# Attention feeding a mixture of experts: v loaded by head pairs, weights and the token plan spread over more steps

## The chip, the core and the metric

The kernel runs on one core of one Trainium2 chip. Five engines work beside each other, each through its own instructions in order: TensorE (PE: matmuls, with its weight loads shown as PEld), VectorE (DVE), ScalarE (ACT), GpSimd (POOL) and SyncE (SP). SP computes nothing here; it issues DMAs. POOL and ACT issue some too. The metric is the device time of one execution in microseconds (us), as the median of several runs.

## The reference

Two layers follow each other. The first is attention with rotary positions, for 8 batches of 8 heads, 576 tokens and 64 columns a head:

```python
q_rot, k_rot = (rotate(q), rotate(k))
scores = scale * np.matmul(q_rot, k_rot.transpose(0, 1, 3, 2))
attn = np.exp(scores - np.max(scores, axis=-1, keepdims=True))
attn = attn / (np.sum(attn, axis=-1, keepdims=True) + 1e-09)
return np.matmul(attn, v)
```

Its output, rearranged to 4608 rows of 512 columns, is the x of the second layer. A dense network of two matrices is applied to every row, and beside it one of 8 experts, picked per row by the largest logit and weighted by its probability:

```python
y_dense = np.maximum(x @ w1_dense, 0.0) @ w2_dense
expert_idx = np.argmax(x @ w_gate, axis=1)
for e in range(E):
    mask = expert_idx == e
    h = np.maximum(x[mask] @ w1[e], 0.0)
    y_moe[mask] = gate_w[mask, None] * (h @ w2[e])
return y_dense + y_moe
```

All expert matrices are 512 x 512. All inputs are float32 in the chip's memory.

## The kernel before

**Pairs and steps.** Attention treats two heads at a time: 8 batches times 4 pairs are 32 pairs. `attention()` runs steps i = 0 to 32 of 9 blocks t = 0 to 8. A step is a software pipeline: it makes the first scores of pair i+2 (`s1_block`, PE, whose row maxima DVE reduces to `negm`, L336), the second scores and exponentials of pair i (`s2_strip`, PE L357, ACT L367), and the product with v of pair i-1 (`av_part`, PE L389). DVE then divides by the sums (`av_scale`: the reciprocal at L400 ends a step, L401 writes x for the batch, and L406 adds up the gate's logits after the last pair of a batch). So L400 runs 32 times, and from one to the next is one step. `s1_block` ends with pair 31 in step 29, so that steps 30 to 32 are lighter.

**What a pair needs.** q and k are loaded by SP for two pairs at a time (`stage_load`, L244 and L247: one large DMA and two small ones), q in even and k in odd steps. `stage_rope` rotates them on POOL (L306 to L309) for pair i+5. `stage_transpose` has SP issue a DMA transpose of the result into `qkT` (L318) for pair i+4. `shift_rows` turns the row maxima of pair i+1 into two rows `mT`, which SP writes into `qkT` (L347, two small DMAs): without these rows `s2_strip` of the next step cannot start. All this stands in one queue on SP, in the order in which the program issues it. In a step that is: the two `mT` rows at t = 1, the transpose at t = 2, then at t = 5 the loads of q or k, of v where there are any, and the store of x.

**v.** `vf` holds v of one batch, eight heads in float32. `stage_v(b)` fills it with one 1 MB DMA (L258) and two small ones for the 64 tail rows (L261). It runs once in the head and then in steps 0, 4, 8 up to 24. ACT casts it pair by pair (`cast_v`, L265).

**x and the weights.** `x_store(b)` writes x of a batch to the chip's memory (`xd`, L415 and L416), on SP in steps 5, 9 and so on; that of the last batch is issued by ACT after the last step. `load_w` has POOL issue a DMA that casts a 512 x 512 matrix to bfloat16 (L222): the dense ones in steps 4 and 6, the eight first expert matrices in steps 8, 10 up to 22, the eight second ones in steps 27 to 29.

**The plan.** The rows of the first 6 batches are sorted into 20 tiles of 128 rows by expert while attention still runs. `gate_steps`, `rank_steps` and `plan_steps` give short pieces of work for DVE, POOL and PE; a dictionary `steps[i, t]` says in which block each piece is issued. `rk[3]` to `rk[5]` are three one-hot products on DVE (`oh`, L510), `pl[4]` and `pl[5]` two further ones with a product on POOL (L578), `mm + [fin]` the matmuls and index arithmetic that end the plan. `fetch(g, ...)` then has POOL gather the tiles of a group by indirect DMA (L756), and SP transpose each (L759). Groups 0, 1 and 2 have 1, 3 and 4 tiles; groups 0 to 2 are fetched in steps 31 and 32, and later ones in the second layer, each two groups ahead.

**The second layer.** `run_groups` goes through the tiles: `dense_in` (PE L789, ACT L791) for a group, `expert_in` (PE L798, ACT L801), a transpose on PE (L807), and `out_tile` (PE L816 and L818, DVE L820), from which POOL scatters the rows to the output (L821). The plan for the last two batches is made on the way, from their logits.

Of the kernel before, what the change touches and what calls it, by code (L numbers as in the profile page):

```python
# [21 lines left out]
P = 128  # L22
# [3 lines left out]
def kernel(  # L26
# [12 lines left out]
    nc = tc.nc  # L39
    B, H, S, D = q.shape  # L40
    N, DG = out.shape
    E = moe_w_gate.shape[1]
# [4 lines left out]
    HP = H // 2  # L47
    NP = B * HP
    MAIN = 512
    TAIL = S - MAIN  # L50
# [170 lines left out]
    def load_w(dst, src):  # L221
        nc.gpsimd.dma_start(dst, src.rearrange("(t p) f -> p t f", p=P))  # L222
# [31 lines left out]
            state["qk", g] = early.tile([P, 2, 2, 10, D], f32, tag="qk", bufs=3, name="qk")  # L254
        load(state["qk", g][:, part], (q, k)[part], b, hh)

    def stage_v(b):
        nc.sync.dma_start(vf.rearrange("p u (a j) d -> p (u a) (j d)", a=2)[:, :, 0:4 * D],  # L258
                          v[b, :, 0:MAIN, :].rearrange("h (p j) d -> p h (j d)", j=4))
        for a in range(2):  # L260
            nc.sync.dma_start(vf[64 * a:64 * a + 64, :, 5 * a + 4, :],  # L261
                              v[b, a::2, MAIN:S, :].rearrange("h p d -> p h d"))

    def cast_v(b, u):
        nc.scalar.copy(v16s[b % VB][:, u, :, VA:VA + 2 * D].rearrange("p n (h d) -> p n h d", d=D),  # L265
# [145 lines left out]
    def x_store(b):  # L411
        r0 = b * S
        xn = state["xn", b]
        eng = nc.scalar if b == B - 1 else nc.sync
        eng.dma_start(xd[r0:r0 + MAIN, :].rearrange("(p j) c -> p j c", j=4), xn[:, 0:4, :])  # L415
        eng.dma_start(xd[r0 + MAIN:r0 + S, :], xn[P - TAIL:P, 4, :])  # L416

    def over_experts(k, wp, dst, src, op):

# [196 lines left out]
    def attention():  # L616
        for i in range(2):
            for t in range(9):
                s1_block(i, t)
                if i == 1 and t == 1:  # L620
                    shift_rows(0)
                    for u in range(HP):
                        cast_v(0, u)
        stage_load(3, 0)
        stage_load(3, 1)
        for i in range(3, RA):
            stage_rope(i)
        stage_transpose(3)
        gt = gate_steps(0, wg)
        rk, got0 = rank_steps(0, wg, attn_sums)  # L630
        steps = {(27, 0): gt[0:1], (27, 2): gt[1:2], (27, 4): gt[2:3]}
        AV = (0, 0), (0, 1), (1, 3), (3, 4), (4, 6), (6, 7), (7, 8), (8, 9), (9, 10)
        state["av"] = av_tile(0)
        for i in range(NP + 1):
            for t in range(9):
                if i + 2 < NP:
                    s1_block(i + 2, t)
                if i < NP:
                    s2_strip(i, t)
                if 1 <= i <= NP and t >= 1:  # L640
                    for k in range(*AV[t]):
                        av_part(i - 1, k)
                    if t == 8:
                        av_scale(i - 1)
                if t == (7 if i == 0 else 5) and i + 1 < NP:
                    v_turn(i + 1)
                if i == 0 and t == 2:
                    v_turn(0)
                if i < NP:
                    t0 = 4 if i == 0 else 1  # L650
                    if t == t0:
                        v_gate(i)
                    if t == t0 + 1:
                        v_split(i)
                if t == 1 and i + 1 < NP:
                    shift_rows(i + 1)
                if t == 2 and i + RA < NP:
                    stage_rope(i + RA)
                if t == 2 and i + LA < NP:
                    stage_transpose(i + LA)  # L660
                if i % HP != 1 and (t in (1, 4) if i % HP == 0 else t == 3):
                    u = 2 + t // 4 if i % HP == 0 else i % HP - 2
                    if 1 <= (i + 2) // HP < B and i < NP - 6:
                        cast_v((i + 2) // HP, u)
                if i in (NP - 6, NP - 5) and t in (1, 4):
                    cast_v(B - 1, 2 * (i - NP + 6) + t // 4)
                if t == 5:

                    g, part = divmod(i + 8, 2)
                    if g < NP // 2:  # L670
                        stage_load(g, part)
                    if i % HP == 0 and i // HP + 1 < B:
                        stage_v(i // HP + 1)
                    if i % HP == 1 and i > HP:
                        x_store(i // HP - 1)
                    if i == 4:
                        load_w(w1d, moe_w1_dense)
                    if i == 6:
                        load_w(w2d, moe_w2_dense)
                    if i % 2 == 0 and 8 <= i < 8 + 2 * E:  # L680
                        load_w(w1e[:, (i - 8) // 2], moe_w1[(i - 8) // 2])
                    if i == 25:
                        route_first()
                    if i == 26:
                        route_ranks()
                        route_tokens()
                    if i == NP - RA:
                        early_cm.__exit__(None, None, None)
                        open_late()
                        wa = late["wa"]  # L690
                        pl, mm, fin = plan_steps(0, wa, attn_sums, got0)
                        w2 = [lambda e=e: load_w(late["w2e"][:, e], moe_w2[e]) for e in range(E)]
                        steps[27, 6] = rk[0:1]
                        steps[27, 7] = w2[0:2]
                        steps[28, 0] = rk[1:2] + pl[0:1]
                        steps[28, 2] = gt[3:4] + w2[2:4]
                        steps[28, 4] = pl[1:2]
                        steps[28, 6] = rk[2:3] + w2[4:6]
                        steps[29, 0] = pl[2:4] + w2[6:8]
                        steps[29, 8] = rk[3:4]  # L700
                        steps[30, 1] = rk[4:5]
                        steps[30, 3] = pl[4:5]
                        steps[30, 5] = rk[5:6]
                        steps[30, 6] = pl[5:6]
                        steps[31, 4] = mm + [fin]
                        steps[31, 6] = [lambda: fetch(0, late["first"], 0, 1), lambda: fetch(1, late["first"], 1, 1)]
                        steps[32, 2] = [lambda: fetch(2, late["first"], 2, 1)]
                for st in steps.pop((i, t), ()):
                    st()
            if i < NP:  # L710
                s2_tails(i, 0)
            if i < NP:
                s2_tails(i, 1)
        assert not steps
        x_store(B - 1)

    def attn_sums(shape):
        t = pp.tile([P, 2, 512], f32, tag="av" if len(shape) == 3 else "s1", bufs=1 if len(shape) == 3 else 2, name="sums")
# [6 lines left out]
    late = {}  # L725
# [37 lines left out]
    with tc.tile_pool(name="attn_sb", bufs=2) as ap, \  # L763
# [3 lines left out]
        with tc.manual_schedule():  # L767
# [6 lines left out]
            nc.gpsimd.tensor_copy(ident_b, ident_f)  # L774
            nc.scalar.copy(ident_h, ident_f)
            for i in range(3):
                stage_rope(i)
                stage_transpose(i)
                if i < 2:
                    stage_load(2, i)  # L780
            pad_tails()
            split_gate()
            stage_v(0)
            attention()

    def dense_in(hd, xs, n, ft):
# [139 lines left out]
```

## Time and profile before

| what | value |
|---|---|
| median of 3 runs | 529.09 us (527.86 to 533.12) |
| the profiled execution | 525.88 us, of which its span, first to last instruction, is 524.1 us |
| PE busy in the span | 417.8 us, 80% |
| DVE busy | 357.9 us, 68% |
| POOL busy | 345.2 us, 66% |
| ACT busy | 283.7 us, 54% |
| mean granted clock of PE | 0.947 |

The steps of attention fill the span from about 41 us to 366 us, the second layer the rest. Busy shares are averages over stages with different limits, so the stages are read apart. In a row of the timeline stand the start, the duration, the engine (with a q where it is only the issue of a DMA), the line, the operation, what it writes and reads, and in brackets how long the engine had been idle and who released it. A row of the table by stretches holds the stretch, its length, for PE, PEld, DVE, ACT and POOL the busy time with the number of instructions, then the granted clock, the share of the 16 DMA engines and the GB/s.

### The profile page before, as it was taken

What the parts mean: (1) busy time and instruction counts of PE and PEld (TensorE: products, weight loads), DVE (VectorE), ACT (ScalarE), POOL (GpSimd) and SP (SyncE); (2) the same over time, 40 slices, a digit from 0 to 9 for tenths busy, and PEclk for the clock granted to TensorE, in tenths of its full rate; (3) what the DMA queues carried; (4) which work ended last, traced back from release to release, by engine and by line L of the source; (5) the groups of instructions that cost most, each with busy time, mean ns of one, the idle gap of its engine ahead of it and who ended that gap; (6) DMA issues with size and microseconds to landing.
All of it is one profiled execution on the core that took longest, in us unless ns stands there. A gap on an engine that the chain in (4) does not pass through costs nothing.

```text
span 524.1 us, 11280 instructions
## 1 busy us (share of the span) xinstructions
PE 417.8 (80%) x4220; PEld 258.0 (49%) x4236; DVE 357.9 (68%) x654; ACT 283.7 (54%) x576; POOL 345.2 (66%) x278
## 2 busy tenths in 40 slices
PE   0177998988798888678988978871789899999993
PEld 0023665655565566455655655550344444444551
DVE  7994999989878989859989998820258523332331
ACT  4007887877677777657887865750333223233320
POOL 4999999889499499875988536155024555555232
PEclk9996999999989999979999987995699999999998
DMA  6498879989979979989997479819215544465222
GB/s 181 90 228 186 222 161 191 236 178 227 184 169 169 246 167 228 180 145 219 194 197 174 102 127 131 158 41 182 66 41 141 141 118 128 139 141 148 76 81 82
DMA packets 151431, 81.41 MB, mean 155 GB/s; under 512 B 112560, under 2 KB 146864, under 8 KB 151376
## 3 DMA queue, kind: packets, MB, share of 16 engines
q1 hardware_dynamic: 136384, 56.33, 49.2%
q0 software_dynamic: 14240, 23.73, 21.6%
q8 instruction: 36, 0.59, 0.5%
q10 hardware_dynamic: 752, 0.61, 0.4%
q14 instruction: 19, 0.16, 0.1%
HBM read 52.05 MB, written 14.42 MB: 127 GB/s over the span
## 4 chain that ended last, share of the span: by engine, by line
PE 44%; DVE 15%; DMA 13%; POOL 9%; ACT 6%; issue 5%; SPq 4%; another core or an unknown queue 3%; POOLq 0%; ACTq 0%; DVEq 0%
DVE negm L336 8%; DMA qkT<-mT 7%; PE pe L798 6%; PE pd L789 6%; PE py L816 6%; PE py L818 6%; PE s L357 4%; PE av L389 4%; PE s L334 4%; ACT pm L367 4%; DMA qk<-in_k_dram 4%; POOL ra L306 3%; POOL nat L309 2%; POOL rb L307 2%
## 5 line engine op out<-in xcount | busy, mean ns | idle before, releaser
L336 DVE TENSOR_REDUCE negm<-s 128x1 f32<-128x576 f32 x288 | 211.0, 751 | 32.8 <-PE s L334 27.2
L367 ACT ACTIVATE pm<-s 128x512 f16<-128x512 f32 x288 | 168.7, 598 | 75.9 <-PE s L357 58.9
L334 PE MATMUL s<-qkT 128*128 128x288 bf16 x512 | 111.1, 301 | 38.5 <-DMA qkT<-nat 23.1
L357 PE MATMUL s<-qkT 128*128 128x64 bf16 (+1 forms) x512 | 113.0, 293 | 19.4 <-DMA qkT<-mT 16.4
L389 PEld LDWEIGHTS <-pm 128*128 128x128 f16 x1600 | 88.8, 99 | 68.3 <-issue 40.5
L389 PE MATMUL av<-v,pm 128*128 128x82 f16 x1600 | 102.7, 202 | 11.5 <-DVE v L292 8.8
L306 POOL TENSOR_TENSOR ra<-qk,cosx 128x1152 bf16<-128x1152 f32 x30 | 79.2, 2640 | 33.3 <-DMA qk<-in_k_dram 20.8
L821 POOL DMA_INDIRECT out_dram<-y,put_i x37 | 36.9, 997 | 84.3 <-DVE y L820 49.4
L309 POOL TENSOR_TENSOR nat<-ra,rb 128x1152 bf16<-128x1152 bf16 x30 | 71.9, 2396 | 2.4
L334 PEld LDWEIGHTS <-qkT 128*128 128x128 bf16 x512 | 40.8, 100 | 55.3 <-DMA qkT<-nat 23.1
L791 ACT ACTIVATE hd<-pd 128x512 bf16<-128x512 f32 (+2 forms) x44 | 23.2, 529 | 69.6 <-PE py L816 32.6
L820 DVE COPY y<-py 128x512 f32<-128x512 f32 x37 | 25.5, 690 | 45.3 <-PE py L818 21.7
L789 PE MATMUL pd<-xs,w1d 128*128 128x512 bf16 (+2 forms) x176 | 41.8, 366 | 14.1 <-ACT hd L791 7.3
L357 PEld LDWEIGHTS <-qkT 128*128 128x128 bf16 x512 | 36.0, 98 | 27.3 <-DMA qkT<-mT 11.5
L801 ACT ACTIVATE hn<-pe,gp 128x512 bf16<-128x512 f32 x37 | 25.4, 687 | 43.9 <-PE pe L798 34.9
L756 POOL DMA_INDIRECT xg<-xd,take_i x37 | 36.6, 988 | 15.1 <-issue 11.0
L809 DVE COPY he<-tr 128x512 bf16<-128x512 bf16 x37 | 15.6, 422 | 43.0 <-PE tr L807 33.7
L307 POOL TENSOR_TENSOR rb<-qk,sinx 128x576 bf16<-128x576 f32 x30 | 42.5, 1416 | 0.0
L308 POOL TENSOR_TENSOR rb<-qk,sinx 128x576 bf16<-128x576 f32 x30 | 42.4, 1414 | 0.0
L798 PE MATMUL pe<-w1e,xs 128*128 x139 | 37.8, 384 | 2.3 <-DVE top L454 1.0
L818 PE MATMUL py<-w2e,he 128*128 x147 | 37.8, 379 | 0.0
L816 PE MATMUL py<-w2d,hd 128*128 128x512 bf16 x142 | 36.7, 379 | 0.3
(170 smaller groups left out, 482.2 us busy)
## 6 DMA issues: line engine op xcount, KB each, us to landing
qk<-in_q_dram SPq DMA_DIRECT2D x16, 512.0 KB
qk<-in_k_dram SPq DMA_DIRECT2D x16, 512.0 KB
vf<-in_v_dram SPq DMA_DIRECT2D x8, 1024.0 KB
w1e<-in_moe_w_dram POOLq DMA_DIRECT2D x8, 512.0 KB
w2e<-in_moe_w_dram POOLq DMA_DIRECT2D x8, 512.0 KB
xd<-xn SPq DMA_DIRECT2D x7, 512.0 KB
qk<-in_q_dram SPq DMA_DIRECT2D x32, 32.0 KB
qk<-in_k_dram SPq DMA_DIRECT2D x32, 32.0 KB
```

The costliest lines, as they stand in the source:

```text
L306: eng.tensor_tensor(a, x, cx, AL.mult)
L307: eng.tensor_tensor(s[:, :, :, 0:half], x[:, :, :, half:D], sx[:, :, :, 0:half], AL.mult)
L309: eng.tensor_tensor(nat[:, :, :, 0:D], a, s, AL.add)
L334: nc.tensor.matmul(ps[:, c, 0:CH], lhsT=qT[:, t * P:(t + 1) * P], rhs=kT[:, k0 + c * CH:k0 + (c + 1) * CH], start=True, stop=True)
L336: nc.vector.tensor_reduce(state["negm", i][:, t:t + 1], ps[:, :, 0:CH], axis=AX.XY, op=AL.max, negate=True)
L357: nc.tensor.matmul(out_ap, lhsT=kT[:, s * P:(s + 1) * P], rhs=qT[:, qa if s < 4 else qb], start=True, stop=True)
L367: nc.scalar.activation(state["pm", i][:, ORDER.index(s), 0:MAIN], ps, AF.Exp, scale=float(scale))
L389: nc.tensor.matmul(state["av"][:, h, x * VC:(x + 1) * VC], lhsT=state["pm", i][:, 4 * h + n if n < 4 else 8, q0:q0 + P], rhs=v16s[b % VB][ ...
L789: nc.tensor.matmul(ps[:, 0:n], lhsT=w1d[:, dt, ft * P:(ft + 1) * P], rhs=xs[:, 0:n, dt, :], start=(dt == 0), stop=(dt == DT - 1))
L798: nc.tensor.matmul(ps, lhsT=xs[:, u, dt, :], rhs=w[:, 0, dt, :], start=(dt == 0), stop=(dt == DT - 1))
L816: nc.tensor.matmul(py, lhsT=hd[:, ft, u], rhs=w2d[:, ft, :], start=(ft == 0), stop=False)
L818: nc.tensor.matmul(py, lhsT=he[:, ft], rhs=w[:, 0, ft, :], start=False, stop=(ft == FT - 1))
```

## The change

- `stage_v` takes a pair: one DMA of two heads and two small ones for their tails. In the head it is called four times; in step 0 twice and in steps 1 to 26 once, always for the next pair in line, so that batch b+1 is loaded over the steps in which batch b is worked on.
- The weights: the first dense matrix is loaded in the head, on POOL ahead of the third rotation; the second in step 1; the first expert matrices in steps 3, 6, 10, 14, 18, 22, 26 and 27; the second ones one or two at a time from step 27, block 6, to step 29, block 5.
- The plan begins in step 25 and not 27. Its pieces stand one to two blocks, or one to two steps, earlier; the first one-hot product moves from step 29, block 8, to step 29, block 2, and the closing matmuls from step 31, block 4, to block 3. Constants are prepared in step 24 and not 25.
- The last `x_store` is issued by SP, in block 8 of step 32, ahead of the fetch of group 2, which moves there from block 2. So four tiles (groups 0 and 1) are fetched in step 31 and four in step 32.

```diff
-    def stage_v(b):
-        nc.sync.dma_start(vf.rearrange("p u (a j) d -> p (u a) (j d)", a=2)[:, :, 0:4 * D],
-                          v[b, :, 0:MAIN, :].rearrange("h (p j) d -> p h (j d)", j=4))
+    def stage_v(b, u):
+        nc.sync.dma_start(vf[:, u].rearrange("p (a j) d -> p a (j d)", a=2)[:, :, 0:4 * D],
+                          v[b, 2 * u:2 * u + 2, 0:MAIN, :].rearrange("h (p j) d -> p h (j d)", j=4))
         for a in range(2):
-            nc.sync.dma_start(vf[64 * a:64 * a + 64, :, 5 * a + 4, :],
-                              v[b, a::2, MAIN:S, :].rearrange("h p d -> p h d"))
+            nc.sync.dma_start(vf[64 * a:64 * a + 64, u, 5 * a + 4, :], v[b, 2 * u + a, MAIN:S, :])
...
-        eng = nc.scalar if b == B - 1 else nc.sync
-        eng.dma_start(xd[r0:r0 + MAIN, :].rearrange("(p j) c -> p j c", j=4), xn[:, 0:4, :])
-        eng.dma_start(xd[r0 + MAIN:r0 + S, :], xn[P - TAIL:P, 4, :])
+        nc.sync.dma_start(xd[r0:r0 + MAIN, :].rearrange("(p j) c -> p j c", j=4), xn[:, 0:4, :])
+        nc.sync.dma_start(xd[r0 + MAIN:r0 + S, :], xn[P - TAIL:P, 4, :])
...
-        steps = {(27, 0): gt[0:1], (27, 2): gt[1:2], (27, 4): gt[2:3]}
+        W1 = (3, 6, 10, 14, 18, 22, 26, 27)
+        steps = {(25, 0): gt[0:1], (26, 0): gt[1:2], (26, 4): gt[2:3], (26, 7): rk[0:1]}
...
-                    if i % HP == 0 and i // HP + 1 < B:
-                        stage_v(i // HP + 1)
+                    for n in range(i, i + 2) if i == 0 else (i + 1,):
+                        if HP <= n + HP < NP:
+                            stage_v(n // HP + 1, n % HP)
...
-                    if i == 4:
-                        load_w(w1d, moe_w1_dense)
-                    if i == 6:
+                    if i == 1:
                         load_w(w2d, moe_w2_dense)
-                    if i % 2 == 0 and 8 <= i < 8 + 2 * E:
-                        load_w(w1e[:, (i - 8) // 2], moe_w1[(i - 8) // 2])
-                    if i == 25:
+                    if i in W1:
+                        load_w(w1e[:, W1.index(i)], moe_w1[W1.index(i)])
+                    if i == 24:
                         route_first()
...
-                        steps[27, 6] = rk[0:1]
-                        steps[27, 7] = w2[0:2]
-                        steps[28, 0] = rk[1:2] + pl[0:1]
-                        steps[28, 2] = gt[3:4] + w2[2:4]
-                        steps[28, 4] = pl[1:2]
-                        steps[28, 6] = rk[2:3] + w2[4:6]
-                        steps[29, 0] = pl[2:4] + w2[6:8]
-                        steps[29, 8] = rk[3:4]
-                        steps[30, 1] = rk[4:5]
-                        steps[30, 3] = pl[4:5]
-                        steps[30, 5] = rk[5:6]
-                        steps[30, 6] = pl[5:6]
-                        steps[31, 4] = mm + [fin]
+                        steps[27, 6] = w2[0:1]
+                        steps[27, 7] = rk[1:2] + pl[0:1]
+                        steps[28, 0] = gt[3:4] + w2[1:2]
+                        steps[28, 3] = pl[1:2] + w2[2:4]
+                        steps[28, 4] = rk[2:3]
+                        steps[29, 0] = pl[2:4] + w2[4:6]
+                        steps[29, 2] = rk[3:4]
+                        steps[29, 5] = w2[6:8]
+                        steps[29, 8] = rk[4:5]
+                        steps[30, 2] = pl[4:5]
+                        steps[30, 4] = rk[5:6]
+                        steps[30, 5] = pl[5:6]
+                        steps[31, 3] = mm + [fin]
                         steps[31, 6] = [lambda: fetch(0, late["first"], 0, 1), lambda: fetch(1, late["first"], 1, 1)]
-                        steps[32, 2] = [lambda: fetch(2, late["first"], 2, 1)]
+                        steps[NP, 8] = [lambda: x_store(B - 1), lambda: fetch(2, late["first"], 2, 1)]
...
-        x_store(B - 1)
...
             for i in range(3):
+                if i == 2:
+                    load_w(w1d, moe_w1_dense)
                 stage_rope(i)
...
-            stage_v(0)
+            for u in range(HP):
+                stage_v(0, u)
             attention()
```

## The prediction

> **What bounds the kernel now.** I read the page first: no engine is busy for more than 80% of the span, so waits matter. Then I cut the span at stage borders (table by stretches).
>
> ```profile
> core 0: us, PE busy (x) PEld busy (x) DVE busy (x) ACT busy (x) POOL busy (x), PEclk, DMA share, GB/s
> 60.20:95.70 35.50, 31.84 (x424) 22.42 (x424) 33.00 (x58) 28.81 (x61) 33.75 (x19) 1.00 0.84 186
> 95.70:289.60 193.90, 162.50 (x2120) 113.20 (x2120) 166.93 (x286) 144.18 (x301) 160.59 (x97) 0.97 0.97 193
> 289.60:349.30 59.70, 49.89 (x617) 34.02 (x618) 48.65 (x108) 41.49 (x88) 26.18 (x41) 0.91 0.62 106
> 349.30:371.00 21.70, 6.16 (x77) 4.29 (x77) 4.93 (x12) 2.08 (x7) 10.50 (x12) 0.66 0.82 174
> 371.00:524.10 153.10, 139.22 (x780) 69.31 (x794) 55.86 (x125) 44.60 (x78) 61.92 (x62) 0.97 0.38 106
> ```
>
> The first stretch is steps 2 to 5, with one weight load: four steps in 35.5 us, DVE busy for 33.0 of them. The second is steps 6 to 25: twenty steps in 193.9 us, 38.8 for four, so 3.3 us more per four and 16.4 in all; there the DMA engines are 97% busy. The last stretch, the second layer, has PE busy for 139 of 153 us, and the change leaves its work alone. The fourth is the seam between the layers: 21.7 us in which every compute engine is nearly idle.
>
> Next I asked what PE waits for in steps 6 to 25 (us, times, longest), how long SP's transposes take there (minimum, median and maximum in ns), and what share of the DMA engines POOL's queue has there, which is weight loads alone.
>
> ```profile
> PE s L357 <- DMA qkT<-mT: 13.4, 8, 4.8
> ```
>
> ```profile
> L318 SPq DMA_TRANSPOSE qkT<-nat x20: 2622/3636/8637, 100.6 to 284.9; - x20
> ```
>
> ```profile
> q0 software_dynamic: 4752, 4.72, 18.5%
> ```
>
> So 13.4 of the 16.4 us are PE waiting for the `mT` rows, which stand in SP's queue. The timeline of SP shows that queue over one step, from the v load of step 12 to the rows of step 14; the fence behind it has the worst meeting, four steps later, with all engines.
>
> ```profile
> 166.56 0.53 SPq L258 DMA_DIRECT2D vf<-in_v_dram  x1
> 167.13 1.25 SPq L261 DMA_DIRECT2D vf<-in_v_dram  x2
> 168.49 1.63 SPq L347 DMA_DIRECT2D qkT<-mT  x2
> 170.22 3.31 SPq L318 DMA_TRANSPOSE qkT<-nat  x1
> 173.58 0.57 SPq L244 DMA_DIRECT2D qk<-in_k_dram  x1
> 174.21 1.37 SPq L247 DMA_DIRECT2D qk<-in_k_dram  x2
> 175.62 0.60 SPq L415 DMA_DIRECT2D xd<-xn  x1
> 176.26 1.45 SPq L416 DMA_DIRECT2D xd<-xn  x1
> 177.81 1.88 SPq L347 DMA_DIRECT2D qkT<-mT  x2
> ```
>
> ```profile
> 213.98 0.80 POOL L222 DMA_DIRECT2D w1e<-in_moe_w_dram  x1
> ...
> 214.74 1.62 SPq L347 DMA_DIRECT2D qkT<-mT  x2
> ...
> 225.36 0.58 PE L357 MATMUL s<-qkT 128*128 128x512 bf16 x1 [4.80 <-DMA qkT<-mT]
> ```
>
> From 166.56 to 177.81 SP has no pause longer than 0.12 us: its queue is as full as the steps are long. At 213.98 a weight load starts, in a step in which SP has just stored x; the rows issued at 214.74 release PE only at 225.36.
>
> **The change part by part.**
>
> *v in pairs, head.* Out goes one issue of three DMAs, in come four: 1.8 us each by the rows at 166.56 and 167.13, so 5.4 us more on SP ahead of the first `mT` rows.
>
> ```profile
> 35.71 1.77 SPq L347 DMA_DIRECT2D qkT<-mT  x2
> ...
> 41.07 0.61 PE L357 MATMUL s<-qkT 128*128 128x512 bf16 x1 [3.03 <-DMA qkT<-mT]
> ...
> 43.20 1.07 ACT L367 ACTIVATE pm<-s 128x512 f16<-128x512 f32 x2
> ```
>
> The rows now leave at 41.1. They land between 1.8 us later (their own issue) and 5.4 (as before, behind the whole of v); I take 3.4, since v drains while it is being issued. PE starts at 44.5, ACT's exponential at 45.1 against 43.20: **+2 us** (0 to 3.9; in the old order ACT's casts of v covered part of this wait). The first weight load, now in the head, puts one issue of 0.8 us on POOL ahead of a rotation that PE needs steps later: nothing.
>
> *v in pairs, steps 0 to 5.* SP carries the 5.4 us and a second pair in step 0 into the first steps. A step without a store now issues rows 1.63, a transpose, q or k 1.94, v 1.78 and about 0.3 of seams: 8.3 us with the quickest transpose, 9.3 with the median one. A step lasts 35.5 / 4 = 8.9, so SP hardly catches up: **+3 us**, an estimate between 0 and 5.4.
>
> *v and weights, steps 6 to 25.* Of nine weight loads there five stay, in steps 6, 10, 14, 18 and 22. One costs 18.5% of 193.9 us over 9, that is 4.0 us of all DMA engines; four fewer free 16 us, 3.2 per four steps. Against that, three more sets of three issues stand in SP's queue per four steps. SP's sum for four steps is then 4 x 5.65 for rows, loads and seams, three transposes at 3.64 and one behind a store at about 5.9 (an estimate between the 3.31 seen and the 8.64), and the store, 1.1: 40.6. If all the 3.2 come off the time for which transposes block SP, it is 37.4. I take the middle, 39.0, against 38.8 now: **+1 us** for five fours (-7 to +9). The five loads that stay fall into just those steps in which SP stores x, so the worst meeting stays.
>
> On this the Trainium skill, page "DMA: Bandwidth & Descriptors", section "Issuing engines are not separate DMA queues", says that the sequencer's time to start a DMA is usually small beside the DMA itself. For the pair's loads it is not: 1.8 us of issue stand against what the row at 186 GB/s moves of 0.29 MB in 1.6. By the page the added issues would cost nothing in the two parts above, and this part's time would fall to the lower end, which is the third rival below.
>
> *The plan.* Its pieces on DVE keep their lengths, and DVE is what steps 27 to 29 wait for (three steps, 298.4 to 333.2, first fence). One of the one-hot products enters step 29.
>
> ```profile
> sum 34.80, DVE 31.40; mean DVE 10.47
> ```
>
> ```profile
> L510 DVE TENSOR_TENSOR oh<-cf,rf x4: 1470/1476/1489, 334.5 to 391.0; 128x1280 f16<-128x1280 f32 x4
> ```
>
> Spreading can win at most the 3.4 us in which DVE idles there; the product costs 1.5; pieces moved to steps 25 and 26 lengthen these by as much as they shorten the others: **-1.5 us** (-3.4 to +1.5). The closing matmuls come one block, 0.9 us, sooner, and with them POOL's gathers.
>
> *The seam.* All engines, in order of time:
>
> ```profile
> 348.26 1.07 POOL L756 DMA_INDIRECT xg<-xd,take_i  x1 [4.17 <-DVE off L596]
> ...
> 351.18 17.00 SPq L759 DMA_TRANSPOSE xs<-xg  x12
> ...
> 366.29 0.22 DVE L400 RECIPROCAL rz<-av 128x10 f32<-128x10 f32 x1 [15.72 <-remote]
> ...
> 368.45 0.45 ACT L791 ACTIVATE hd<-pd 128x128 bf16<-128x128 f32 x2 [17.40 <-DMA xs<-xg]
> ...
> 370.81 0.59 PE L798 MATMUL pe<-w1e,xs 128*128 x1 [1.03 <-DVE top L454]
> ```
>
> DVE waits 15.7 us for PE's last product with v while twelve gathers and twelve transposes run; what held PE the trace doesn't say. Behind that DVE stands the last store of x, on ACT's queue, and behind the store ACT's first work for the second layer, at 368.45. After the change ACT is free, and SP stops after four transposes, since the store in its queue waits for DVE. If it is gathers and transposes together that hold PE, it is free when the four are done: at 351.2 + 17.0 x 4/12 = 356.9, and with some 1.6 for landing at 358.5. ACT follows at once, and the first expert 2.4 later (370.81 - 368.45), at 361: **-9.6 us**. The next eight transposes wait for the store, about 2.2 later, and their first four end at 366.4, in time for the third group, whose turn comes some 7 us after the first expert. If gathers alone hold PE, only the 0.9 and about 2 of ACT's queue are won: -2.9. I take the first, since PE's trouble begins with the first transposes. POOL gains nothing by the later fetch: its gathers follow each other without a wait anyway.
>
> **Sum** against the execution's own 525.88: +2 + 3 + 1 - 1.5 - 9.6 = -5.1, so 520.8. The median stands 3.2 above that execution: **524 us**.
>
> **The rivals.**
>
> 1. *SP's queue becomes the bound* (slower). For it: the queue without a pause. Against: SP's time shrinks with the DMA load. It decides from where four steps' issues exceed 38.8 us. With none of the 3.2 saved they are 40.6, and with a second transpose of 5.9 per four steps 42.9; at the middle, 41.7, the steady part costs 14.5 and not 1, and the first steps the full 5.4 and not 3: -5.1 + 13.5 + 2.4 = +11, 540 us.
> 2. *The seam's stall stays*, since gathers alone make it. For it: DVE is released two transposes before the last. Against: the first gathers alone left PE running. -5.1 + 6.7 = +1.6: 531 us, no change.
> 3. *The issues are hidden* and only the relief remains: 0 + 0 - 7 - 1.5 - 9.6 = -18, 511 us. For it: 97% DMA share now against 84% in steps with one weight load, which had no excess. Against: rows that leave late in the head.
>
> **How the numbers follow.** Chances: forecast 0.37, rival 1 0.27, rival 2 0.25, rival 3 0.11. About 1% (5 us) is what a measurement of this kernel can tell from no change. The forecast, give or take 6, lies half beyond -1%; rival 3 wholly; rivals 1 and 2 hardly: faster 0.31. Rival 1 and a little of rival 2 are slower: 0.29. The rest, 0.40, is within. The range 511 to 541 cuts half of rival 3 and the far half of rival 1.
>
> **What would show it.** Right: PE's first strip near 44.5; steps 6 to 25 near 195 us, with PE's waits for the rows still at the stores of x; POOL's queue near 10% there; DVE's last reciprocal near 358, and ACT's first dense piece right behind. Wrong: that reciprocal still 18 us behind the first gather (rival 2); SP without any pause and each four steps above 40 us (rival 1); steps of 8.9 from the start (rival 3). Weights landing too late for the first expert would overturn all of it.

## The result and the profile after

The changed kernel takes 547.18 us (544.84 to 548.58) where the kernel before took 528.48 beside it (520.88 to 533.12): a ratio of 1.043, with 1.029 to 1.057 as its interval. Ratios leave out executions more than 1.5% above the fastest of their kernel, so 1.043 is not that of the two medians, and two later kernels (v in batches, and the first of those without the costs) have profiles of such executions (1.7% and 1.8% above), whose stages are, if anything, too long. It is slower, above the range of 511 to 541. Run once more in a later set it took 545.82 beside 528.79, a ratio of 1.035 (1.029 to 1.042).

The view by stretches of the changed kernel, cut at the reciprocals that end steps 1, 5, 25, 31 and 32 (columns as in the prediction):

```profile
0.00:67.20 67.20, 30.06 (x206) 15.50 (x207) 49.92 (x70) 23.26 (x46) 54.77 (x54) 0.97 0.73 162
67.20:107.60 40.40, 34.31 (x424) 23.61 (x424) 33.32 (x59) 29.09 (x62) 27.72 (x16) 0.92 0.77 171
107.60:305.40 197.80, 166.46 (x2120) 115.94 (x2120) 166.56 (x287) 144.79 (x301) 156.31 (x93) 0.95 0.82 179
305.40:371.60 66.20, 51.92 (x622) 34.91 (x622) 53.65 (x107) 42.10 (x88) 33.93 (x46) 0.90 0.72 126
371.60:387.30 15.70, 5.39 (x60) 3.32 (x59) 1.31 (x4) 0.92 (x3) 9.72 (x11) 0.67 0.63 129
387.30:544.30 157.00, 142.16 (x792) 70.72 (x806) 59.64 (x134) 45.94 (x82) 61.92 (x62) 0.95 0.42 114
```

Beside the same view of the kernel before, and with a second pair of profiles (both kernels again, on one chip), in us:

| stage | before | after | difference | second pair | predicted |
|---|---|---|---|---|---|
| head, to the first reciprocal | 60.2 | 67.2 | +7.0 | 59.4, 66.8: +7.4 | +2 |
| steps 2 to 5 | 35.5 | 40.4 | +4.9 | 35.5, 39.8: +4.3 | +3 |
| steps 6 to 25 | 193.9 | 197.8 | +3.9 | 197.0, 198.5: +1.5 | +1 |
| steps 26 to 31 | 59.7 | 66.2 | +6.5 | 60.7, 65.7: +5.0 | -1.5 |
| step 32 (the seam) | 17.0 | 15.7 | -1.3 | 16.8, 15.5: -1.3 | -9.6 with the next row |
| second layer | 157.8 | 157.0 | -0.8 | 158.8, 156.7: -2.1 | |
| span | 524.1 | 544.3 | +20.2 | 528.2, 543.0: +14.8 | -5.1 |

For steps 6 to 25 the changed kernel's waits (us, times, longest), SP's transposes (minimum, median, maximum in ns) and POOL's DMA queue read:

```profile
PE s L356 <- DMA qkT<-mT: 13.9, 5, 4.5
...
L317 SPq DMA_TRANSPOSE qkT<-nat x21: 2717/2767/6042, 105.8 to 300.7; - x21
...
q0 software_dynamic: 2640, 2.62, 10.2%
```

POOL's share fell from 18.5% to 10.2%, and the median transpose from 3.64 us to 2.77, as much as the most favourable end of the forecast had it. PE nevertheless waits as long for its rows as before, 13.9 against 13.4 us. Added up from SP's timeline, its issues cover about 190 of these 197.8 us, with two pauses of more than 0.3 us, 1.5 in all; in the kernel before they covered 175 of 193.9, with seven such pauses, 11.3 in all. v's issues rose from 12 to 37 us, the transposes fell from 84 to 70: the queue's pauses over the twenty steps are all but used up.

### The profile page after: what moved, and what is told of

Read it like the earlier page. It is cut to its first block, busy times and chain, and to the rows that moved or that the text cites. A ratio compares the mean times of both kernels' runs of the same rounds, so it can differ in the third digit from the quotient of the medians.

```text
span 544.3 us, 11371 instructions
## 1 busy us (share of the span) xinstructions
PE 430.3 (79%) x4220; PEld 264.0 (48%) x4236; DVE 364.4 (67%) x654; ACT 286.1 (53%) x576; POOL 344.4 (63%) x278
## 4 chain that ended last, share of the span: by engine, by line
PE 48%; DVE 13%; DMA 11%; POOL 10%; issue 7%; ACT 6%; SPq 4%; POOLq 0%; another core or an unknown queue 0%; ACTq 0%
DVE negm L335 8%; PE pd L789 7%; DMA qkT<-mT 6%; PE pe L798 6%; PE av L388 6%; PE py L816 6%; PE py L818 6%; PE s L356 5%; PE s L333 5%; ACT pm L366 4%; DMA qk<-in_k_dram 3%; POOL nat L308 3%; POOL ra L305 3%; SPq L317 2%; POOL rb L306 2%
## 5 line engine op out<-in xcount | busy, mean ns | idle before, releaser
L333 PE MATMUL s<-qkT 128*128 128x288 bf16 x512 | 114.9, 310 | 45.3 <-DMA qkT<-nat 27.3
L356 PE MATMUL s<-qkT 128*128 128x64 bf16 (+1 forms) x512 | 115.8, 298 | 27.4 <-DMA qkT<-mT 23.8
L388 PEld LDWEIGHTS <-pm 128*128 128x128 f16 x1600 | 92.6, 102 | 77.1 <-issue 49.8
L388 PE MATMUL av<-v,pm 128*128 128x82 f16 x1600 | 107.9, 207 | 17.5 <-issue 9.3
L305 POOL TENSOR_TENSOR ra<-qk,cosx 128x1152 bf16<-128x1152 f32 x30 | 79.3, 2643 | 44.5 <-DMA qk<-in_k_dram 31.6
L333 PEld LDWEIGHTS <-qkT 128*128 128x128 bf16 x512 | 41.8, 102 | 63.8 <-DMA qkT<-nat 27.3
L356 PEld LDWEIGHTS <-qkT 128*128 128x128 bf16 x512 | 36.5, 100 | 35.2 <-DMA qkT<-mT 17.9
```

The costliest lines, as they stand in the source:

```text
L305: eng.tensor_tensor(a, x, cx, AL.mult)
L333: nc.tensor.matmul(ps[:, c, 0:CH], lhsT=qT[:, t * P:(t + 1) * P], rhs=kT[:, k0 + c * CH:k0 + (c + 1) * CH], start=True, stop=True)
L356: nc.tensor.matmul(out_ap, lhsT=kT[:, s * P:(s + 1) * P], rhs=qT[:, qa if s < 4 else qb], start=True, stop=True)
L388: nc.tensor.matmul(state["av"][:, h, x * VC:(x + 1) * VC], lhsT=state["pm", i][:, 4 * h + n if n < 4 else 8, q0:q0 + P], rhs=v16s[b % VB][ ...
```

## The experiments

The stages below come from the same view. Chips differ (see the seam), so ratios are to the kernel before on the same chip.

**Were it v's issues or the weights?** First the changed kernel with v as before:

```diff
-    def stage_v(b, u):
+    def stage_v(b):      # one DMA of a batch and two small ones, as in the kernel before
...
-            for u in range(HP):
-                stage_v(0, u)
+            stage_v(0)
```

> The changed kernel, with v loaded a whole batch at a time, as in the kernel before; weights, plan and seam as in the changed one. Theory A (the added issues on SP are what the early steps and the head lose): first rows about 5 us earlier (39.2), step 2 from 13.4 to about 9, and the twenty steps from 197.8 to about 190, since the four weight loads less are then gain: in all 13 to 17 us, about 532. Theory B (the weight loads, now in the steps that store x and in step 1, are the cost): only the head's 5 us, step 2 stays above 12 and the twenty steps above 196: about 542.

It took 512.67 us where the kernel before took 520.71: 0.979 (0.967 to 0.990). The 532 of theory A is no measure here: on this chip step 32 takes 2.7 us and not 15.7 (see the seam).

Then the two halves alone, each in the kernel before:

```diff
-                    if i % HP == 0 and i // HP + 1 < B:
-                        stage_v(i // HP + 1)
+                    for n in range(i, i + 2) if i == 0 else (i + 1,):
+                        if HP <= n + HP < NP:
+                            stage_v(n // HP + 1, n % HP)
```

> The kernel before, with v loaded in pairs as the change does it, and nothing else of the change. Theory A (the added issues on SP cost by themselves): first rows 4 to 5 us later than before, step 2 above 11 us, the twenty steps above 200 (193.9 before), in all 15 to 25 us slower than the kernel before. Theory B (they cost only together with the moved weight loads): head 5 us later, twenty steps within 3 us of 193.9, in all 5 to 8 us slower.

```diff
-                    if i == 4:
+                    if i == 1:
+                        load_w(w2d, moe_w2_dense)
+                    if i == 2:
                         load_w(w1d, moe_w1_dense)
-                    if i == 6:
-                        load_w(w2d, moe_w2_dense)
-                    if i % 2 == 0 and 8 <= i < 8 + 2 * E:
-                        load_w(w1e[:, (i - 8) // 2], moe_w1[(i - 8) // 2])
+                    if i in W1:
+                        load_w(w1e[:, W1.index(i)], moe_w1[W1.index(i)])
```

> The kernel before, with the weight loads spread as the change spreads them (the first dense matrix in step 2, the second in step 1, the experts' in steps 3, 6, 10, 14, 18, 22, 26 and 27) and nothing else. Theory A (weights and v add): the twenty steps 6 to 25 take 184 to 190 us where the kernel before takes 193.9 and 197.0; 4 to 10 us faster than the kernel before. Theory B (what the last experiments won they won by the plan or the store): twenty steps above 193, time unchanged. Its seam is that of the kernel before, so it also shows whether this chip has the stall: last step 15 to 17 us, or 2.7.

v in pairs alone: 545.56 beside 528.79, 1.032 (1.025 to 1.039). Weights alone: 511.28 beside 517.55, 0.988 (0.978 to 0.997). The twenty steps 6 to 25 of these three, v in pairs first, then weights, then the changed kernel with v in batches:

```profile
104.50:310.30 205.80, 170.09 (x2120) 117.89 (x2120) 166.61 (x287) 145.23 (x301) 161.01 (x97) 0.92 0.89 183
```

```profile
96.20:281.80 185.60, 161.95 (x2120) 113.67 (x2120) 165.99 (x286) 144.30 (x301) 162.51 (x96) 0.98 0.89 191
```

```profile
98.90:283.00 184.10, 159.51 (x2120) 111.95 (x2120) 165.88 (x288) 143.83 (x301) 154.90 (x93) 1.00 0.95 193
```

| steps 6 to 25, us | weights as before | weights spread |
|---|---|---|
| v in batches | 193.9, 197.0 | 185.6, 184.1; later kernels 189.7, 186.4 |
| v in pairs | 205.8 | 197.8, 198.5; six later kernels 193.9 to 202.5 |

By the first profiles of a cell, v in pairs costs 9 to 14 us down a column, and the spread weights win 7 to 13 along a row. These mix chips, and one kernel varies by some us. But 197.0, 205.8, 189.7 and 198.5 were all taken on one chip: there v in pairs costs 8.8 us in either column and the spread weights win 7.3 in either row. The granted clock differs between the rows (0.92 to 1.00), but steps without a wait last 8.4 or 8.5, 8.8 and 9.8 us in all of them, so it isn't the clock. PE's wait for its rows there, in the same order as the three rows above, with the transposes of v in pairs alone:

```profile
PE s L356 <- DMA qkT<-mT: 18.7, 5, 5.0
...
L317 SPq DMA_TRANSPOSE qkT<-nat x20: 2697/2824/7558, 112.4 to 305.6; - x20
```

```profile
PE s L357 <- DMA qkT<-mT: 5.9, 4, 2.0
```

```profile
PE s L357 <- DMA qkT<-mT: 6.3, 3, 2.4
```

So theory A holds in all three runs, for the size of the twenty steps. Step 2 was told right by the first run (8.4 us, as before the change), not by v in pairs alone: there step 2 stays 8.4 and step 5 takes 13.6. The debt of the first steps is the same, 40.7 - 35.5 = 5.2 us; only where it is paid moves.

**The head.** The first load goes behind the third rotation:

```diff
                 if i == 2:
-                    load_w(w1d, moe_w1_dense)
...
+            load_w(w1d, moe_w1_dense)
             pad_tails()
```

> The changed kernel, with the first weight load in the head behind the third rotation on POOL and not ahead of it. Theory A (the load shifts POOL's rotation against DVE's, and the two engines block each other): DVE's third instruction of the first rotation goes from 6.3 us back to about 3.2, the first `mT` rows leave SP at 40.7 and not 44.2, and the first reciprocal comes 3 to 3.5 us earlier: about 543.5. Theory B (the issues of v alone made the head late): rows at 44 as now, time unchanged at 547.

537.04 us beside 520.71: 1.037 (1.029 to 1.045), no better than the changed kernel. In the changed kernel DVE's first rotation stands so against POOL's (timeline, in order of start):

```profile
12.69 0.96 POOL L222 DMA_DIRECT2D w1d<-in_moe_w_dense_dram  x1
13.27 6.33 DVE L307 TENSOR_TENSOR rab<-qk,sinx 128x576 bf16<-128x576 f32 x1
13.67 2.64 POOL L305 TENSOR_TENSOR ra<-qk,cosx 128x1152 bf16<-128x1152 f32 x1
16.23 1.41 POOL L306 TENSOR_TENSOR rb<-qk,sinx 128x576 bf16<-128x576 f32 x1
17.58 1.40 POOL L307 TENSOR_TENSOR rb<-qk,sinx 128x576 bf16<-128x576 f32 x1
...
36.90 0.58 SPq L258 DMA_DIRECT2D vf<-in_v_dram  x1
...
44.23 1.76 SPq L346 DMA_DIRECT2D qkT<-mT  x2
```

and with the load behind the rotation:

```profile
13.27 3.16 DVE L307 TENSOR_TENSOR rab<-qk,sinx 128x576 bf16<-128x576 f32 x1
...
18.36 2.87 SPq L317 DMA_TRANSPOSE qkT<-nat  x1
...
22.90 0.98 POOL L222 DMA_DIRECT2D w1d<-in_moe_w_dense_dram  x1
...
25.09 6.64 SPq L317 DMA_TRANSPOSE qkT<-nat  x1
...
44.71 1.76 SPq L346 DMA_DIRECT2D qkT<-mT  x2
```

Theory A is right about DVE: its third instruction is back from 6.33 to 3.16 us. But the rows leave no sooner, since the load now runs beside the second transpose, which takes 6.64 us where the first took 2.87 (with v in pairs alone, begun at the same time, the second took 2.77). Theory B's number came true by another way. What the load costs in the head is seen in the first reciprocal: 60.2 and 59.4 in the kernel before, 63.8 with v in pairs alone, 63.4 with the load in the head and v in batches, 67.2 and 66.8 with both, 60.8 with neither (weights alone, the load in step 2).

On DVE's 6.33 us, the Trainium skill, page "SBUF — State Buffer", section "Who interferes with whom", says that a DVE instruction with two inputs in SBUF contends with a GpSimd instruction that reads SBUF, and that the order of issue decides which of the two blocks. The trace agrees that one holds the other, but not on which: DVE's instruction, done in 0.80 us for the second pair and here recorded to start 0.40 us ahead of POOL's first, waited through three of POOL's.

**The plan.** Its first pieces go behind the last rotation on POOL:

```diff
-        steps = {(25, 0): gt[0:1], (26, 0): gt[1:2], (26, 4): gt[2:3], (26, 7): rk[0:1]}
+        steps = {(26, 3): gt[0:1], (26, 6): gt[1:2], (26, 7): gt[2:3], (26, 8): rk[0:1]}
```

> The changed kernel, with the first four pieces of the plan in step 26, blocks 3, 6, 7 and 8, so that on POOL the subtraction `ex` (L442) stands behind the rotation of the last pair. Theory A (POOL's queue): in the changed kernel POOL waited 12.5 us at `ex` with two rotations behind it, and step 26 took 16.9 us. With `ex` behind them that wait costs nobody anything: step 26 takes 9 to 10 us, the span falls by about 7, the time to about 540. Theory B (SP's queue and the two weight loads of steps 26 and 27 hold these steps): step 26 stays above 14 us and the time within 2 us of 547.

The changed kernel's timeline of POOL and DVE around steps 25 and 26, in order of start:

```profile
286.45 0.11 POOL L182 MEMSET keep<- 128x8 f32 x1
...
298.57 0.39 DVE L419 TENSOR_REDUCE mx<-lgs 128x30 f32<-128x240 f32 x1
299.04 0.60 POOL L442 TENSOR_TENSOR ex<-lgs,mx 128x240 f32<-128x240 f32 x1 [12.47 <-DMA vf<-in_v_dram]
299.60 2.62 POOL L305 TENSOR_TENSOR ra<-qk,cosx 128x1152 bf16<-128x1152 f32 x1
...
305.41 0.21 DVE L399 RECIPROCAL rz<-av 128x10 f32<-128x10 f32 x1
307.48 2.70 POOL L305 TENSOR_TENSOR ra<-qk,cosx 128x1152 bf16<-128x1152 f32 x1
308.16 2.05 DVE L452 TENSOR_SCALAR top<-top 128x30 f32<-128x30 f32 x1
...
313.72 2.06 DVE L455 TENSOR_TENSOR hs<-hit,top 128x240 f32<-128x240 f32 x1
...
319.34 0.18 DVE L202 TENSOR_SCALAR pi<-tok 128x40 int32<-128x40 int32 x1 [2.99 <-POOL tok L199]
...
320.33 0.41 PE L333 MATMUL s<-qkT 128*128 128x288 bf16 x2 [3.13 <-DVE negm L335]
...
322.29 0.21 DVE L399 RECIPROCAL rz<-av 128x10 f32<-128x10 f32 x1
```

The plan's first subtraction, `ex`, needs the maxima of batch 5, which DVE has at 298.96. The bracket names a DMA of v, which `ex` does not read; what it reads is `mx`, from the row above. Issued in step 25, block 0, it stands on POOL ahead of two rotations, and POOL, done with everything else at 286.6, waits 12.47 us. The first of them begins 13 us late, at 299.60, and the second, pushed behind it to 307.48, meets the plan's next pieces: `top` and `hs`, 0.18 and 0.60 us in the kernel before, take 2.05 and 2.06, `top` until POOL's `ra` ends at 310.2, `hs` beside the end of this last rotation; `pi` waits 3.0 for POOL's `tok`, which stands behind the rotations and a load; and the row maxima queued behind `pi` hold PE for 3.1. Step 26 takes 16.9 us (reciprocal to reciprocal), against 8.8 before.

With `ex` behind the rotations, steps 26 to 31 are again as long as before the change, 59.4 us, and step 26 takes 11.7:

```profile
310.30:369.70 59.40, 47.58 (x614) 32.19 (x614) 50.02 (x107) 41.26 (x88) 25.93 (x43) 0.97 0.82 138
```

```profile
POOL ex L442 <- DVE mx L419: 3.2, 1, 3.2
```

The time is 532.7 beside 520.71, 1.022 (1.013 to 1.031). Theory A, with 6.8 of the 7 us, though step 26 keeps 2 us more than it said. (Its 540 us is no measure, since on this chip step 32 takes 2.7; four other kernels, with these pieces where the change has them, took 64.4 to 66.5 us here for the six steps.)

**The seam.** The store of the last x goes on POOL ahead of group 2's gathers, so that eight of twelve gathers wait for the last product with v:

```diff
-        nc.sync.dma_start(xd[r0:r0 + MAIN, :]...
+        eng = nc.gpsimd if b == B - 1 else nc.sync
+        eng.dma_start(xd[r0:r0 + MAIN, :]...
```

> The changed kernel, with the last store of x issued by POOL and not SP, ahead of the fetch of group 2, so that POOL's last eight gathers wait for DVE's last product. Theory A (the gathers alone hold PE): the last reciprocal comes 5 to 6 us behind the one before it and not 15.7, and the second layer is no longer than now (153 us): about 538. Theory B (the eight gathers hold PE just as much when they run beside the first matmuls of the second layer): the reciprocal comes early, but the second layer is 7 to 10 us longer and the time stays at 545 to 547. Theory C (transposes and gathers together hold PE, or something else in the seam): the reciprocal stays 14 us or more behind.

537.68 beside 520.71, 1.037 (1.030 to 1.043): no gain. But in all four kernels of that set step 32 took 2.6 or 2.7 us, also in those that left the seam alone. So both kernels were profiled again:

> The kernel before, unchanged, profiled beside the next three. In four kernels that leave the seam's instructions as they are, or move only the last store, the last step was 2.7 us and not 15.7. Theory A (the seam's stall is a matter of the chip or of the run, not of the program): here too the last step is below 6 us, and the time about 512 to 520. Theory B (the stall belongs to the program of before, by its twelve gathers and transposes in a row): 15 us or more, as in the first profile.

> The changed kernel, unchanged, profiled beside the kernel before on this chip. Theory A: last step below 6 us, all else as in its first profile (step 2 above 11, step 26 near 17, twenty steps near 198), time about 535 to 540. Theory B: last step 15 us or more. By both it is 3.5 to 5% slower than the kernel before.

529.9 and 545.82 us, with step 32 at 16.8 and 15.5 again: theory B's number. But the set with 2.7 ran on one chip and this one on another, and the weights alone, whose seam is that of the kernel before, had 2.7 back on the first. So it is the chip that has the stall or not, as theory A has it, though its number for this run was wrong. What the stall costs in the end is step 32 and the second layer together: 172.2 to 175.6 us in the six profiles that have it, 161.3 to 165.6 in the seven of the chip without, so 8 to 11 us for like seams. The first set's chip ran the kernel before in 520.7 and 517.6, this one in 528.8. The held gathers came twice more; first on the chip without the stall:

> The changed kernel, with the last store of x on POOL ahead of group 2's gathers, once more, since the chip of its first run had no stall in the seam. If this chip has it: by theory A (gathers hold PE) the last step is 5 to 7 us and not 15.5, and PE issues without gaps from the end of the fourth gather on; by theory C (not the gathers) it is 14 us or more. Without the stall it tells nothing.

535.28 us, step 32 at 2.7: it tells nothing. Then on a third chip, where the kernel before takes 531.2, together with a kernel that holds back all twelve gathers:

```diff
-                        steps[31, 6] = [lambda: fetch(0, ...), lambda: fetch(1, ...)]
-                        steps[NP, 8] = [lambda: x_store(B - 1), lambda: fetch(2, ...)]
+                        steps[NP, 8] = [lambda: x_store(B - 1), lambda: fetch(0, ...),
+                                        lambda: fetch(1, ...), lambda: fetch(2, ...)]
```

> The changed kernel, with the last store of x on POOL ahead of group 2's gathers: the third time, for a chip that has the seam's stall (where the kernel before takes about 528 us and not 518). Theory A (gathers hold PE): last step 5 to 7 us, PE's gaps end with the fourth gather. Theory C: 14 us or more. On a chip without the stall (last step 2.7 by both) it tells nothing.

> The changed kernel, with the last store of x on POOL ahead of all twelve gathers, so that none runs beside the last product with v. On a chip with the stall: theory A (gathers hold PE): last step below 3.5 us, but the first dense piece comes 5 to 8 us behind the last reciprocal, and PE has gaps between its first instructions of the second layer as long as gathers run; theory C (a place in PE's program is slow, whatever POOL does): last step 14 us or more. Without the stall: last step 2.7, the second layer 5 us longer.

In the changed kernel PE issues by ones and twos between gaps long after SP's four transposes are done, at 378.1, and until the last gather is issued:

```profile
372.35 5.78 SPq L756 DMA_TRANSPOSE xs<-xg  x4
...
382.75 0.36 PE L388 MATMUL av<-v,pm 128*128 128x82 f16 x3 [1.20 <-issue]
383.42 0.95 POOL L753 DMA_INDIRECT xg<-xd,take_i  x1 [0.30 <-issue]
385.58 0.23 PE L388 MATMUL av<-v,pm 128*128 128x82 f16 x1 [2.46 <-issue]
...
387.26 0.22 DVE L399 RECIPROCAL rz<-av 128x10 f32<-128x10 f32 x1 [14.36 <-PE av L388]
```

With eight gathers held (third chip):

```profile
374.13 0.94 POOL L754 DMA_INDIRECT xg<-xd,take_i  x1 [0.30 <-issue]
374.50 0.69 PE L388 MATMUL av<-v,pm 128*128 128x82 f16 x14 [0.94 <-issue]
...
376.18 0.69 PE L388 MATMUL av<-v,pm 128*128 128x82 f16 x14 [0.48 <-issue]
...
376.90 0.22 DVE L399 RECIPROCAL rz<-av 128x10 f32<-128x10 f32 x1 [3.25 <-PE av L388]
```

With all twelve held:

```profile
373.32 2.02 PE L388 MATMUL av<-v,pm 128*128 128x82 f16 x50
...
389.13 2.77 PE L790 MATMUL pd<-xs,w1d 128*128 128x384 bf16 x8
...
392.13 0.95 POOL L754 DMA_INDIRECT xg<-xd,take_i  x1 [0.31 <-issue]
395.19 0.87 ACT L792 ACTIVATE hd<-pd 128x384 bf16<-128x384 f32 x2 [5.12 <-remote]
```

In step 32 PE's gaps go with the gathers: with four beside it, the step takes 4.6 us (5 to 7 were expected); with none, the fifty products run without a gap in 2.0. They don't go with the transposes, the fourth of which is over at 378.1 in the changed kernel while the gaps go on. Nor is it the clock: in the six profiles with the stall it was 0.64 to 0.73 in step 32, and with all twelve held 1.00, too little to make 15 us of 2.7. But gathers do not hold PE at every place. With all twelve held, PE's eight products at 389.13 run beside them one every 0.35 us, without a gap; what comes late is ACT's work on these products, after 5.1 us of waiting and past the last gather, and its bracket names no engine, only `remote`. What is held is partly lost again. The second layer takes 162.1 us with eight held and 170.8 with twelve (157.0 in the changed kernel). Not all of the 5.1 us from 157.0 to 162.1 need be the held gathers' doing: on the chip without the stall the second layer takes 158.6 to 162.9 us, with gathers held or not. Step 32 and the second layer together: 172.7 in the changed kernel, 166.7 with eight held, 173.5 with twelve. Theory A holds for step 32, with half of the gain given back, and all of it with all twelve held; the gaps that it expected of PE in the second layer did not come. These are single runs, and the changed kernel itself was not run on the third chip: that this chip has the stall is read from these gaps and from the time of the kernel before.

**What is left when the costs are taken out.** v in batches and the plan's first pieces behind the last rotation, as above, and the first load in step 2; then the same with eight gathers held:

```diff
                 if i == 2:
-                    load_w(w1d, moe_w1_dense)
...
+                    if i == 2:
+                        load_w(w1d, moe_w1_dense)
                     if i in W1:
```

> The changed kernel without the parts that cost: v a whole batch at a time, the first weight load in step 2 and not in the head, and the first four pieces of the plan in step 26 behind the last rotation. Kept are the spread weight loads and the later pieces of the plan. Theory A (the three costs are separate and add): first reciprocal at 60 to 61, steps 2 to 25 at 8.4 to 9.8 but for two or three, step 26 below 12: about 7 to 10 us below the kernel with v in batches (512.7), so 503 to 506. Theory B (what is saved in one place is waited for in the next, since DVE is busy for 33 of 35.5 us): within 3 us of 512.7.

> The kernel with v in batches, the first load in step 2 and the plan's first pieces behind the last rotation, and now also with the last store of x on POOL ahead of group 2's gathers. If the chip has the seam's stall: theory A (gathers hold PE, and little is given back) 8 to 10 us less than without the held gathers, the ratio to the kernel before 0.955 to 0.965 instead of 0.974; theory B (the eight gathers then hold the first pieces of the second layer) the same ratio of 0.974, with the second layer 8 us longer. Without the stall: 0.97 to 0.98.

516.25 us beside 528.79, 0.974 (0.968 to 0.980), on the chip with the stall, and 507.71 beside 517.55, 0.982 (0.972 to 0.993), on the one without. Both beat the kernel before beside them, and the first the changed kernel too (545.82 on its chip). The 503 to 506 us of theory A came from the chip without the stall, so on the other neither theory's number can be judged; the second's 0.982 lies just above the 0.97 to 0.98 expected without the stall. The first reciprocals are at 60.5 and 59.2, so the head's cost is gone; steps 26 to 31 take 61.1 and 62.2 us, no less than before. Against the weights alone (0.988, 0.978 to 0.997) the intervals overlap: so no gain beyond that of the weights is shown, and none by the later plan pieces. Whether the held gathers win anything in this kernel on a chip with the stall wasn't tried.

## Why the prediction was wrong

Three steps of the prediction failed: the first weight load, priced at nothing (3.2 us), the plan, forecast at -1.5 us (+6.5), and the seam, forecast at -9.6 (-2.1). The other terms came out inside their ranges, though mostly near the dear end.

**What bounds the kernel.** Right: DVE is busy for about 166 us of steps 6 to 25 in every variant, and in all of them PE waits there for the `mT` rows in SP's queue (5.9 to 18.7 us).

**v in pairs, head.** Right in its steps, a little low in the end. With v in pairs alone the timeline shows

```profile
40.83 1.76 SPq L346 DMA_DIRECT2D qkT<-mT  x2
```

```profile
43.67 0.61 PE L356 MATMUL s<-qkT 128*128 128x512 bf16 x1 [5.24 <-DMA qkT<-mT]
```

where the forecast had 41.1 and 44.5. The first reciprocal is 3.6 us later than before (63.8 against 60.2), not 2, but within the 0 to 3.9; one of the 3.6 arises behind PE's start. In the changed kernel the rows left at 44.23, and the 3.4 us between are the load.

**The first load in the head, priced at nothing.** This step failed outright: 3.2 us (63.4 against 60.2; 2.6 and 4.2 against 60.8 and 59.2, two kernels without it on the same chip). "A rotation that PE needs steps later" looked at who waits for POOL's result, not at who is running beside POOL: DVE's rotation of the first pair, which everything waits for, was held through three of POOL's instructions.

**v in pairs, steps 0 to 5.** +3 was the middle of 0 to 5.4; the upper end came, 4.9, and 5.2 for v alone. SP's sum for a step had been 8.3 to 9.3 against a step of 8.9: a queue with next to no slack, so nothing was caught up.

**Steps 6 to 25.** Forecast +1, measured +3.9 and +1.5: the sum held, and so did its two terms. They were +9 for the issues (40.6 against 38.8, five times) and -8 for the lighter weight queue (half of 3.2, five times); on the one chip they measured +8.8 and -7.3. Worked out again from the rows: three added sets of 1.8 us are 5.4 per four steps; four transposes shorter by 3.64 - 2.82 give 3.3 back, in the run with v in pairs alone; 2.1 for four steps, 10 for twenty, of 9 to 12 measured. So v in pairs by itself shortened the transposes, which the forecast did not have; against that, less of the queue's slack was used up than it had counted on (SP idled for 18.7 us of the twenty steps before, and still for 12.5 with v in pairs alone). That +9 came out so closely is in part luck. That the issues cost, and not the smaller transfers as such, rests on this sum: v was not tried on another engine's queue. Two slips in the prediction's sums change nothing: SP's terms add up to 40.5 and not 40.6, and the seam's times to 360.9 and -9.9. The Trainium skill's rule (page "DMA: Bandwidth & Descriptors", section "Issuing engines are not separate DMA queues"), that the time to start a DMA is usually small beside the DMA, would make v in pairs free; here it costs 9 to 12 us in twenty steps.

**The plan.** The second step that failed: -1.5 forecast, +6.5 measured. DVE's pieces were counted by their lengths and POOL's queue not at all. An instruction that waits, put ahead of two rotations, gave away the 12 us by which POOL was ahead. With it behind them the term is -0.3: the gain that was forecast did not come either.

**The seam.** The third: -9.6 forecast, -2.1 measured (-3.4 in the second pair), the -2.9 of rival 2 nearly to the number. That the gathers of group 2 "follow each other without a wait anyway" stood in the prediction; that they would then hold PE just as long was the conclusion to draw, and the choice between gathers and transposes was made by when the trouble begins and not by when it ends.

**The rivals.** Rival 2 came true in its place, with its sign: the last reciprocal 17.8 us behind the first gather. Rival 1 named SP's queue, with 540 us the nearest price; of its two marks, SP without any pause came nearly true (1.5 us of pauses in 197.8), and each four steps above 40 us was missed narrowly (197.8 / 5 = 39.6). None held the two costs that were priced at nothing or less, 3.2 + 8.0 of the 25 us between forecast and execution.

## What to carry to other kernels

Splitting a transfer into more DMAs is paid on the issuing queue: count the issues against that queue's slack, and where it has little, as here, expect to pay: nearly the full sum in the first steps (4.9 and 5.2 of 5.4 us), later what shorter transposes did not give back (9 to 12 of 27). Before an instruction that waits is moved forward, list what stands behind it on its own engine, and on two engines that work on the same memory count who is running at that moment, not only who needs the result. A term that comes out near zero as the difference of two large ones is two experiments, each of which may be worth having alone: the spread weights alone were a gain.

## What was not expected of the hardware

- The seam's stall is a matter of the chip: 15.5 to 17.1 us for step 32 in six profiles (the first two, and four on one chip), 2.6 or 2.7 in seven on another, four of them with all gathers where they were. On a third the step took 4.6 us with eight gathers held back and 2.7 with all twelve. Why PE is held at this place while gathers are issued, on one chip and not on another, stays open.
- One DVE instruction of 0.8 us was held for 6.33 us by three of POOL's in a row, so the engine that is blocked need not come next.
- A DMA transpose of 2.8 us took 6.64 when a weight load began 2.2 us ahead of it.
